# A talking-heads attention with a gated feed-forward: first tile in another order, every second block's first head mixing in three fp32r products

## The chip, the cores and the metric

The kernel runs on one core of a Trainium2 chip. The metric is the device time in microseconds of one execution. TensorE (PE) multiplies, PEld is its weight load, DVE (VectorE), ACT (ScalarE) and POOL (GpSimd) work element by element, and SP (SyncE) issues most DMAs. Each engine runs its own instructions strictly in the order in which they were written; between engines there are semaphores.

## The reference

There are 4 batches, 12 heads, 448 positions and 64 numbers per head. All inputs and the output are fp32, except that the two large weights arrive as 64-bit floats.

```python
scores = scale * np.matmul(q, k.transpose(0, 1, 3, 2))
scores = np.einsum('bhij,hg->bgij', scores, w_pre)
scores = scores - np.max(scores, axis=-1, keepdims=True)
attn = np.exp(scores)
attn = attn / (np.sum(attn, axis=-1, keepdims=True) + 1e-09)
attn = np.einsum('bhij,hg->bgij', attn, w_post)
x = np.matmul(attn, v)              # then to 1792 tokens x 768
h = x @ w_in                        # 768 x 2048
g = np.where(h >= 1, h, np.where(h <= -1, 0, (h + 1) ** 2 / 4))
out = g @ w_out                     # 2048 x 768
```

## The kernel before

The attention is cut into 16 tiles of up to 120 query rows (120, 120, 120 and 88 in each batch). `scores` (L143 to L165) multiplies a tile's queries with the keys of two pairs of heads, in three fp32r products per head: queries and keys had been split into a high part (rounded to fp32r) and the low rest, which `trans_k` and `trans_q` make when they transpose. A `scores` call leaves four PSUM banks, and ACT copies one of them to `ssb` (L160), DVE three (L164).

A *block* is 10 query rows of a tile with all 12 heads, so 120 rows (108 for some) by 448 keys: `load_s` (L179, a DMA on SP) gathers them from `ssb`, `pre` (L185) mixes the heads with one fp32 product whose stationary side is `wpre`, a 120 x 120 matrix that holds w_pre ten times along its diagonal. The profile shows this product as two instructions. `row_max` (L189, DVE), `exps` (L195, ACT) and `norm` (L201 and L202 on DVE, then `wr` on POOL, L206) make the softmax, `post` (L216, ACT copy L218) does the second mixing, and `pv` (L232) multiplies with the values.

Blocks go in 48 *groups*: 36 of four blocks and 12 of three. The main loop has one *step* per group, and in step n it writes, in this order: the `load_s` of group n+1, all `pre` of group n, all `row_max`, all `exps`, `norm`, some work of a weight conversion (`convs`, L267 to L286, spread over ACT, DVE and POOL), `post` of group n-1, transposes for coming tiles (`trans_k` in nine of the steps, whose casts L125 and subtractions L128 are DVE's), `pv`, a `scores` call, and a list of late items. The late items of steps 44 to 47 are the first work of the feed-forward: `load_x` (L382, three buffers `xr`) and `split_x` (L390 on ACT, L391 on DVE) for its first 512 tokens, and `load_w` (L353, L355). SP's queue is in order: a DMA that must wait for a buffer holds up all behind it.

PSUM has six banks `ps_l`, used in turn by `pre`, `post`, the transposes, `pv` and half of `scores`, and two banks `ps_q`.

Before the loop stands the first tile: loads of q and k (L101, L110), transposes with small `warm` products (L499) between them, three `scores` calls, the `load_s` of group 0. After it come 64 steps of the feed-forward (`ffn1` L404, `gate`, `ffn2` L441), with fp32r products throughout; the change does not touch them.

Of the kernel before, what the change touches and what calls it, by code (L numbers as in the profile page):

```python
# [9 lines left out]
F32 = mybir.dt.float32  # L10
# [5 lines left out]
ALU = mybir.AluOpType  # L16
# [6 lines left out]
def tile_talking_heads_moe(  # L23
# [119 lines left out]
    def scores(t, hps):  # L143
# [6 lines left out]
        for u, hp in enumerate(hps):  # L150
# [6 lines left out]
            (rest if u else todo).append((2 * hp, ps[0]))  # L157
# [23 lines left out]

    def pre(m):
        k = blocks[m][2] * H
        lps[m] = ps_l.tile([128, S], F32, tag="l", name="ps_l")
        nc.tensor.matmul(out=lps[m], lhsT=wpre[:k], rhs=s10.pop(m)[:k], start=True, stop=True)  # L185

    def row_max(m):
        nm = ap_.tile([128, 1], F32, tag="nm", name="nm", bufs=8)
# [271 lines left out]
    with tc.manual_schedule():  # L460
        load_q(0, (0,))
        k0 = [ap_.tile([KP, 2, KC, 2, D], F32, tag=f"v{g}", name=f"k0{g}", bufs=1) for g in range(3)]
# [14 lines left out]
        wrep = const.tile([128, 2, H], F32, name="wrep")  # L477
        nc.vector.memset(wrep, 0.0)
        for n, w in enumerate((w_pre, w_post)):
            nc.scalar.dma_start(out=wrep[:KM, n, :], in_=w.unsqueeze(0).to_broadcast([IB, H, H]))  # L480

        wpre = const.tile([128, 128], F32, name="wpre")
        wpost = const.tile([128, H, IB], F32, name="wpost")
        nc.vector.memset(wpre, 0.0)

        nc.vector.scalar_tensor_tensor(
            out=wpre[:, :KM].rearrange("p (i g) -> p i g", g=H),
            in0=mask.unsqueeze(2).to_broadcast([128, IB, H]), scalar=float(D) ** -0.5,
# [198 lines left out]
```

## Time and profile before

| what | value |
|---|---|
| median of 3 runs | 975.99 us (975.35 to 978.43) |
| the profiled execution | 973.09 us, its span 971.4 us |
| PE busy | 947.6 us, 98% of the span |
| DVE, ACT, POOL busy | 57%, 53%, 17% |
| first `pre` / last `pre` of the attention | 32.35 us / 477.14 us from the span's start |
| mean granted clock of TensorE | 0.993 of full speed |

The span is what the trace covers; 1.7 us of the execution lie around it. A matmul's busy time overlaps the next one's, so the cost of a matmul in a row is the distance from its start to the start of the next. Times in the rows below are from the start of the span.

### The profile page before, as it was taken

Reading aid. Unit: us, or ns where it says so; the run is one execution under the profiler, and the core shown is the slowest. Engines: PE = TensorE matmul, PEld = TensorE weight load, DVE = VectorE, ACT = ScalarE, POOL = GpSimd, SP = SyncE. Lnnn points to the kernel's source line nnn. Section 1 sums busy time; section 2 is a strip of 40 time slices with the busy share of each in tenths; the row PEclk is TensorE's granted clock in tenths of the full one; section 3 lists DMA queues with packets and bytes.
Section 4 is the critical chain, followed back from the end, with each engine's and each line's share of the span. In section 5 each row is a group of like instructions: output and inputs, shape, how many; then the busy total and the mean of one; then the engine's idle time right before and its main releaser. Section 6 shows DMA issues by size and latency. Waiting matters only on the chain.

```text
span 971.4 us, 17796 instructions
## 1 busy us (share of the span) xinstructions
PE 947.6 (98%) x6698; PEld 775.7 (80%) x6698; DVE 554.7 (57%) x997; ACT 517.9 (53%) x1097; POOL 169.2 (17%) x253
## 2 busy tenths in 40 slices
PE   7999999999999999999899999999999999999997
PEld 6667777777778787777688877888888888888997
DVE  3665756666665756654355566554454644545774
ACT  2566577666676666665555454443333533334553
POOL 0134233323333233422201212000000000000000
PEclk8999999999999999999999999999999999999999
DMA  5685657775667856653544432020000200000100
GB/s 88 177 240 163 198 177 216 212 211 176 198 199 218 218 173 206 191 196 107 166 163 140 149 128 87 11 98 1 1 23 1 92 1 1 12 1 6 65 2 33
DMA packets 118362, 115.22 MB, mean 119 GB/s; under 512 B 61700, under 2 KB 107268, under 8 KB 118276
## 3 DMA queue, kind: packets, MB, share of 16 engines
q1 hardware_dynamic: 115232, 113.37, 38.4%
q10 hardware_dynamic: 3044, 0.70, 0.5%
q8 instruction: 54, 0.88, 0.4%
q14 instruction: 32, 0.26, 0.1%
HBM read 55.85 MB, written 19.66 MB: 78 GB/s over the span
## 4 chain that ended last, share of the span: by engine, by line
PE 91%; DMA 3%; DVE 2%; ACT 1%; issue 1%; POOL 1%; ACTq 0%; SPq 0%; POOLq 0%
PE o L441 22%; PE ps_h L404 22%; PE ps_l L185 15%; PE ps_a L216 15%; PE ps_x L232 8%; PE ps_s L155 7%; DMA s<-ssb 2%; PE ps_w L499 1%; PE ps_k L121 1%; PE ps_t L138 1%; POOL wo L286 1%; DMA k<-in_k_dram 1%; DMA wi<-wid 0%; DVE mx L418 0%; DVE mx L417 0%
## 5 line engine op out<-in xcount | busy, mean ns | idle before, releaser
L216 PEld LDWEIGHTS ps_a<-wr,e 128*112 128x112 f32 x1440 | 154.6, 177 | 18.5 <-issue 18.5
L195 ACT ACTIVATE e<-ps_l,nm 128x448 f32<-128x448 f32 x180 | 113.0, 632 | 94.3 <-DVE nm L189 93.7
L206 POOL TENSOR_SCALAR wr<-wpost,rs 128x120 f32<-128x120 f32 x180 | 103.2, 591 | 337.1 <-DVE rs L202 290.4
L185 PE MATMUL ps_l<-s,wpre 120*128 120x448 f32 x360 | 150.3, 559 | 6.6 <-DMA s<-ssb 6.6
L216 PE MATMUL ps_a<-wr,e 128*112 128x120 f32 (+1 forms) x1440 | 155.3, 266 | 0.0
L404 PE MATMUL ps_h<-xh,wil 128*128 128x512 f32 (+1 forms) x384 | 139.5, 363 | 0.0
L404 PE MATMUL ps_h<-xl,wih 128*128 128x512 f32 (+1 forms) x384 | 139.2, 363 | 0.0
L404 PE MATMUL ps_h<-xh,wih 128*128 128x512 f32 (+1 forms) x384 | 139.2, 362 | 0.0
L185 PEld LDWEIGHTS ps_l<-s,wpre 120*128 120x128 f32 x360 | 64.6, 191 | 72.2 <-issue 62.0
L441 PE MATMUL o<-woh,gl 128*128 128x512 f32 x448 | 115.7, 339 | 4.4 <-DVE gl L421 4.4
L189 DVE TENSOR_REDUCE nm<-ps_l 128x1 f32<-128x448 f32 x180 | 105.1, 618 | 21.1 <-PE ps_l L185 16.0
L441 PE MATMUL o<-woh,gh 128*128 128x512 f32 x448 | 115.6, 339 | 0.0
L441 PE MATMUL o<-wol,gh 128*128 128x512 f32 x448 | 115.2, 339 | 0.0
L417 DVE TENSOR_TENSOR mx<-ps_h,a 128x512 f32<-128x512 f32 (+1 forms) x64 | 39.9, 624 | 120.6 <-ACT a L416 120.6
L164 DVE COPY ssb<-ps_s 120x448 f32<-120x448 f32 (+1 forms) x144 | 82.6, 619 | 44.3 <-PE ps_s L155 41.4
L416 ACT ACTIVATE a<-ps_h,c 128x512 f32<-128x512 f32 (+1 forms) x64 | 40.5, 633 | 113.5 <-PE ps_h L404 113.4
L218 ACT ACTIVATE aT<-ps_a 112x480 f32<-112x480 f32 x180 | 96.0, 591 | 4.9 <-PE ps_a L216 3.6
L441 PEld LDWEIGHTS o<-woh,gl 128*128 128x128 f32 x448 | 75.1, 189 | 17.9 <-DVE gl L421 6.8
L420 ACT ACTIVATE gh<-mx 128x512 fp32r<-128x512 f32 (+1 forms) x64 | 37.0, 578 | 92.5 <-DVE mx L418 92.5
L441 PEld LDWEIGHTS o<-wol,gh 128*128 128x128 f32 x448 | 76.3, 188 | 10.0
L441 PEld LDWEIGHTS o<-woh,gh 128*128 128x128 f32 x448 | 76.4, 188 | 9.7
L232 PE MATMUL ps_x<-aT,v 112*64 112x120 f32 (+1 forms) x1536 | 83.8, 262 | 0.0
(66 smaller groups left out, 1246.5 us busy)
## 6 DMA issues: line engine op xcount, KB each, us to landing
s<-ssb SPq DMA_DIRECT2D x172, 210.0 KB
wraw<-in_moe_w_in_dram SPq DMA_DIRECT2D x32, 384.0 KB
raw<-in_moe_w_out_dram SPq DMA_DIRECT2D x20, 384.0 KB
wid<-wt SPq DMA_DIRECT2D x32, 192.0 KB
wi<-wid SPq DMA_DIRECT2D x16, 384.0 KB
v<-in_v_dram SPq DMA_DIRECT2D x12, 448.0 KB
out_dram<-osb SPq DMA_DIRECT2D x14, 384.0 KB
wraw<-in_moe_w_out_dram SPq DMA_DIRECT2D x12, 384.0 KB
```

Of the source, the lines that this page charges most:

```text
L155: nc.tensor.matmul(out=ps[s][:n], lhsT=qt[t][x][r, hp, :n], rhs=kt[b, hp][y][r, :], start=(m == 0), stop=(m == 2))
L164: nc.vector.tensor_copy(out=ssb[t][:n, h, :], in_=x[:n])
L185: nc.tensor.matmul(out=lps[m], lhsT=wpre[:k], rhs=s10.pop(m)[:k], start=True, stop=True)
L189: nc.vector.tensor_reduce(out=nm, in_=lps[m], axis=AX.X, op=ALU.max, negate=True)
L195: nc.scalar.activation(out=e, in_=ps, func=AF.Exp, bias=nm, accum_out=sm[:, j:j + 1])
L206: nc.gpsimd.tensor_scalar_mul(out=w[:, :, :ni], in0=wpost[:, :, :ni], scalar1=rs[:, j:j + 1])
L216: nc.tensor.matmul(out=ps[:, r, :ni * H], lhsT=e[:, r * KP:(r + 1) * KP], rhs=w[:, :, :ni], start=True, stop=True)
L218: nc.scalar.activation(out=aT[t][:, :, :, c:c + ni], in_=ps[:, :, :ni * H].rearrange("q r (h i) -> q r h i", h=H), func=AF.Copy)
L232: nc.tensor.matmul(out=ps[s * D:(s + 1) * D, m, :n], lhsT=vt[b, g][:, 2 * m + s, r * D:(r + 1) * D], rhs=a[:, r, 4 * g + 2 * m + s, :n], s ...
L404: nc.tensor.matmul(out=ps[:, :n], lhsT=w[:, kk, :], rhs=x[:, :n], start=(c == 0), stop=(c == last))
L416: nc.scalar.activation(out=a[:, :n], in_=ps[:, :n], func=AF.Relu, scale=0.5, bias=c05)
L441: nc.tensor.matmul(out=o[bank][:, c0:c0 + ne], lhsT=g[:, t * 128:(t + 1) * 128], rhs=w[:, e0:e0 + ne], start=(f == 0 and m == 0 and c0 == ...
```

## The change

Five edits:

- Every second block of a group (`groups[n + 1][1::2]`: two of four, one of three; 82 blocks in all, since group 0 has no step before it) is no longer mixed by one fp32 product. In the step before, DVE makes `sh`, its fp32r value, and `sl`, the rest (new `split`, two instructions); `pre` then takes three fp32r products with `wpre_h` and `wpre_l`. One split stands between `row_max` and `exps`/`norm` of the step, the other after `norm`. `load_s` issues these blocks first.
- A `scores` call has two of its four copies on ACT and two on DVE.
- The first tile: the key loads of pairs 3 to 5 on ACT's queue, all others on SP's; ACT's table load ahead of them; the loads of w_pre and w_post on SP; the transposes of all key pairs ahead of the three `scores` calls, with fewer `warm` products; `wpre` and `wpost`, with the split of `wpre`, after the copies of the scores.
- `load_x` and `split_x` of the first 512 tokens at other steps: no load in step 45, loads 3 and 4 in step 46, load 5 in step 47.
- Tiles of 128 partitions that used 120 have 120.

```diff
 def load_k(b, hp, t=None):
-            (nc.scalar if first and s else nc.sync).dma_start(...)
+            (nc.scalar if first and hp > 2 else nc.sync).dma_start(...)
 def scores(t, hps):
-            (rest if u else todo).append((2 * hp, ps[0]))
+            todo.append((2 * hp, ps[0]))
...
+    def split(m):
+        k = blocks[m][2] * H
+        x = s10.pop(m)
+        hi = ap_.tile([KM, S], F32R, tag="sh", name="sh", bufs=2)
+        lo = ap_.tile([KM, S], F32R, tag="sl", name="sl", bufs=2)
+        nc.vector.tensor_copy(out=hi[:k], in_=x[:k])
+        nc.vector.tensor_tensor(out=lo[:k], in0=x[:k], in1=hi[:k].bitcast(F32), op=ALU.subtract)
+        s10[m] = (hi, lo)
...
+        if isinstance(x, tuple):
+            for j, (w, y) in enumerate(((wpre_h, x[0]), (wpre_l, x[0]), (wpre_h, x[1]))):
+                nc.tensor.matmul(out=lps[m], lhsT=w[:k], rhs=y[:k], start=(j == 0), stop=(j == 2))
+        else:
+            nc.tensor.matmul(out=lps[m], lhsT=wpre[:k], rhs=x[:k], start=True, stop=True)
...
         for hp in range(1, HP):
-            warm(3)
+            warm(2)
             trans_k(0, hp)
-            if hp in (3, 5):
-                warm(2)
-                scores(0, [hp - 3, hp - 2])()
-        warm(4)
-        scores(0, [4, 5])()
+        for g in range(3):
+            scores(0, [2 * g, 2 * g + 1])()
...
-        for kk in range(KDM):
-            put(NE + 1 + kk // 2, lambda kk=kk: split_x(0, kk))
-            if kk + 3 < KDM:
-                put(NE + 1 + kk // 2, lambda kk=kk: load_x(0, kk + 3))
+        for w0, loads, splits in ((1, (), (0, 1)), (2, (3, 4), (2,)), (3, (5,), (3, 4, 5))):
...
-                for m in groups[n + 1]:
+                for m in (*groups[n + 1][1::2], *groups[n + 1][::2]):
                     load_s(m)
...
+            nxt = list(groups[n + 1][1::2]) if n + 1 < NG else []
             for m in ms:
                 row_max(m)
+            if nxt:
+                split(nxt.pop(0))
             for j, m in enumerate(ms):
                 if j == 3:
                     post(old.pop(0)) if old else None
                 exps(m, j, sm)
             if ms:
                 norm(ms, sm)
+            for m in nxt:
+                split(m)
             convs(share * (n + 0.4))
```

On PE, the first mixing of group 1 with what stands before and behind it. Before (`s_...` are the gathered blocks, `ps_s` the scores):

```order
L155 MATMUL ps_s_415<-kl_186,qh 120x448
L185 MATMUL ps_l<-s_334,wpre 128x448
L185 MATMUL ps_l<-s_336,wpre 128x448
L185 MATMUL ps_l<-s_338,wpre 128x448
L185 MATMUL ps_l<-s_340,wpre 128x448
L216 MATMUL ps_a<-wr,e 112x120 x16
```

and now:

```order
L155 MATMUL ps_s_412<-kl_179,qh 120x448
L200 MATMUL ps_l<-s_326,wpre 120x448
L198 MATMUL ps_l<-sh,wpre_h 120x448
L198 MATMUL ps_l<-sh,wpre_l 120x448
L198 MATMUL ps_l<-sl,wpre_h 120x448
L200 MATMUL ps_l<-s_328,wpre 120x448
L198 MATMUL ps_l<-sh,wpre_h 120x448
L198 MATMUL ps_l<-sh,wpre_l 120x448
L198 MATMUL ps_l<-sl,wpre_h 120x448
L231 MATMUL ps_a<-wr,e 112x120 x16
```

Two of the four fp32 products became three fp32r products each, and PE now goes from fp32 to fp32r and back twice inside the group.

On DVE, step 0 (group 0, with the splits for group 1). Before:

```order
L189 TENSOR_REDUCE nm<-ps_l 128x1 x4
L201 TENSOR_SCALAR rs<-sm 128x4
L202 RECIPROCAL rs<-rs 128x4
L141 TENSOR_TENSOR ql<-ps_t,qh 128x360
L164 COPY ssb<-ps_s_390 120x448
```

and now:

```order
L204 TENSOR_REDUCE nm<-ps_l 120x1 x4
L187 CAST sh<-s_322 120x448
L188 TENSOR_TENSOR sl<-s_322,sh 120x448
L216 TENSOR_SCALAR rs<-sm 120x4
L217 RECIPROCAL rs<-rs 120x4
L187 CAST sh<-s_324 120x448
L188 TENSOR_TENSOR sl<-s_324,sh 120x448
L141 TENSOR_TENSOR ql<-ps_t,qh 128x360
L164 COPY ssb<-ps_s_386 120x448
```

The splits stand ahead of `rs` and ahead of the transposes' and scores' copies, and each waits for a `load_s` of its own step.

On SP, the DMAs of steps 45 and 46 (`s_...` for group 47 are the last three gathers). Before:

```order
L382 DMA xr<-xd 128x512 x2
L353 DMA wi_5949<-wid 128x768
L355 DMA wo_5950<-wod 128x768
L179 DMA s_5953<-ssb 120x1x448
L179 DMA s_5955<-ssb 108x1x448
L179 DMA s_5957<-ssb 108x1x448
```

and now:

```order
L368 DMA wi_6417<-wid 128x768
L370 DMA wo_6418<-wod 128x768
L179 DMA s_6421<-ssb 108x1x448
L179 DMA s_6423<-ssb 120x1x448
L179 DMA s_6425<-ssb 108x1x448
L263 DMA xd<-xo 768x1x120
L397 DMA xr<-xd 128x512 x2
```

The two loads of `xr` went behind the last gathers.

## Rows read from the trace of the kernel before

**Rows 1.** The page: busy time, share of the span and instructions of two engines, and the lines of the chain that ended last, by share of the span.

```profile
PE 947.6 (98%) x6698; PEld 775.7 (80%) x6698; DVE 554.7 (57%) x997; ACT 517.9 (53%) x1097; POOL 169.2 (17%) x253
...
PE o L441 22%; PE ps_h L404 22%; PE ps_l L185 15%; PE ps_a L216 15%; PE ps_x L232 8%; PE ps_s L155 7%; DMA s<-ssb 2%; PE ps_w L499 1%; PE ps_k L121 1%; PE ps_t L138 1%; POOL wo L286 1%; DMA k<-in_k_dram 1%; DMA wi<-wid 0%; DVE mx L418 0%; DVE mx L417 0%
```

**Rows 2.** Busy time by stretch, one whole step (18, which has transposes of keys): the stretch, its length, then busy time and count on PE, PEld, DVE, ACT and POOL, granted clock, DMA share, GB/s.

```profile
201.39:212.13 10.74, 10.74 (x98) 8.40 (x96) 7.86 (x17) 6.70 (x19) 3.24 (x5) 1.00 0.65 189
```

**Rows 3.** The weight loads of one group's `pre` in order of time (start, length, engine, line, operation): the first two, the third, and the first load of `post` behind them. Between the third and the last stand five more of L185.

```profile
306.49 0.30 PEld L185 LDWEIGHTS ps_l<-s,wpre 120*128 120x128 f32 x2 [0.31 <-issue]
306.97 0.19 PEld L185 LDWEIGHTS ps_l<-s,wpre 120*128 120x128 f32 x1 [0.19 <-ACT wk L273]
...
309.23 0.18 PEld L216 LDWEIGHTS ps_a<-wr,e 128*112 128x112 f32 x1 [0.19 <-issue]
```

**Rows 4.** fp32r matmuls of the feed-forward in order of time: the first and the last of 17 in a row with 512 columns, the first and the last of 17 with 256 columns, and the last two pairs of a `scores` call (448 columns, two heads side by side).

```profile
565.40 0.39 PE L404 MATMUL ps_h<-xl,wih 128*128 128x512 f32 x1
...
569.03 0.39 PE L404 MATMUL ps_h<-xh,wih 128*128 128x512 f32 x1
...
929.58 0.28 PE L404 MATMUL ps_h<-xh,wil 128*128 128x256 f32 x1
...
931.49 0.28 PE L404 MATMUL ps_h<-xl,wih 128*128 128x256 f32 x1
...
305.99 0.37 PE L155 MATMUL ps_s<-kh,ql 64*120 64x448 f32 x2
306.20 0.36 PE L155 MATMUL ps_s<-kl,qh 64*120 64x448 f32 x2
```

**Rows 5.** Weight loads where `pv` (fp32, 112 rows by 64 columns) is followed by `pre` (fp32, 120 rows by 128 columns): the first two of `pre`, and the third.

```profile
466.05 0.30 PEld L185 LDWEIGHTS ps_l<-s,wpre 120*128 120x128 f32 x2 [0.16 <-issue]
466.53 0.19 PEld L185 LDWEIGHTS ps_l<-s,wpre 120*128 120x128 f32 x1 [0.19 <-issue]
```

**Rows 6.** Groups by line and form (count, busy us and mean ns of one, idle time before), of DVE: three kinds of operation that are like a split's two, and the copy of the scores. Then, from the views of single lines, shortest, median and longest ns of L282 (DVE, two inputs from SBUF) and of L206 (POOL).

```profile
L276 DVE TENSOR_SCALAR wt<-wt 128x384 int32<-128x384 int32 x44 | 15.2, 347 | 0.0
L125 DVE CAST kh<-ps_k 128x448 fp32r<-128x448 f32 x18 | 11.2, 620 | 7.1 <-PE ps_k L121 7.1
L391 DVE TENSOR_TENSOR xl<-xr,xh 128x512 fp32r<-128x512 f32 x18 | 11.8, 688 | 19.9 <-ACT xh L390 19.9
L164 DVE COPY ssb<-ps_s 120x448 f32<-120x448 f32 x108 | 61.9, 620 | 23.4 <-PE ps_s L155 23.4
...
L282 DVE SCALAR_TENSOR_TENSOR wt<-wraw,wt x44: 557/559/687, 46.6 to 422.8; 128x384 int32<-128x384 int32 x44
...
L206 POOL TENSOR_SCALAR wr<-wpost,rs x180: 552/585/663, 37.5 to 484.6; 128x120 f32<-128x120 f32 x172, 128x108 f32<-128x108 f32 x8
```

**Rows 7.** DVE in step 18 in order of time (start, length; in brackets the idle time before it and what ended it), and SP's issues of the gathers in that step.

```profile
203.41 2.21 DVE L189 TENSOR_REDUCE nm<-ps_l 128x1 f32<-128x448 f32 x4
207.18 0.17 DVE L201 TENSOR_SCALAR rs<-sm 128x4 f32<-128x4 f32 x1 [1.57 <-ACT e L195]
...
208.37 0.62 DVE L125 CAST kh<-ps_k 128x448 fp32r<-128x448 f32 x1 [0.81 <-PE ps_k L121]
...
211.66 1.72 DVE L164 COPY ssb<-ps_s 88x448 f32<-88x448 f32 x3 [0.37 <-PE ps_s L155]
...
201.35 3.52 SPq L179 DMA_DIRECT2D s<-ssb  x4
```

**Rows 8.** The start in order of time: ACT's first work, PE behind it, the last transposes of keys, the last copies of scores, the first gathers, the first `pre`; and a piece of the chain that ended last, from step 2.

```profile
0.78 6.26 ACTq L101 DMA_DIRECT2D k<-in_k_dram  x6
...
10.23 1.28 ACT L140 ACT_TABLE_LOAD   x1 [10.23 <-DMA k<-in_k_dram]
12.84 1.65 PE L499 MATMUL ps_w<-ident 128*128 128x128 f32 x6 [4.71 <-DVE ql L141]
...
21.89 0.55 PE L121 MATMUL ps_k<-ident,k 112*128 112x112 f32 x4
...
2.72 7.63 SPq L101 DMA_DIRECT2D k<-in_k_dram  x5
...
26.49 1.69 DVE L164 COPY ssb<-ps_s 120x448 f32<-120x448 f32 x3 [0.95 <-PE ps_s L155]
28.27 3.47 SPq L179 DMA_DIRECT2D s<-ssb  x4
32.35 2.04 PE L185 MATMUL ps_l<-s,wpre 120*128 120x448 f32 x5
...
52.00 8.12 DMA s<-ssb
```

**Rows 9.** Steps 46 and 47 in order of time: SP's `xr` loads and last gathers, DVE's first `split_x`, and PE's `pre` of group 46 and of group 47; and the busy time by stretch there (columns as in Rows 2).

```profile
467.81 0.92 SPq L382 DMA_DIRECT2D xr<-xd  x2
...
469.78 2.82 SPq L179 DMA_DIRECT2D s<-ssb  x3
...
467.09 1.29 DVE L391 TENSOR_TENSOR xl<-xr,xh 128x512 fp32r<-128x512 f32 x2 [4.08 <-ACT xh L390]
...
466.05 2.52 PE L185 MATMUL ps_l<-s,wpre 120*128 120x448 f32 x6
...
477.14 4.19 PE L185 MATMUL ps_l<-s,wpre 120*128 120x448 f32 x6 [4.32 <-DMA s<-ssb]
...
470.00:480.00 10.00, 5.68 (x48) 3.76 (x47) 2.26 (x5) 4.36 (x12) 1.71 (x3) 0.87 0.93 268
```

More of the change, by code (lines that the diff above doesn't have):

```diff
@@ L100, in load_k @@
         for s in range(2):
-            (nc.scalar if first and s else nc.sync).dma_start(out=t[:, :, s, :], in_=k[b, 2 * hp + s].rearrange("(p r) d -> p r d", r=KC))
+            (nc.scalar if first and hp > 2 else nc.sync).dma_start(out=t[:, :, s, :], in_=k[b, 2 * hp + s].rearrange("(p r) d -> p r d", r=KC))
         kraw[b, hp] = t
@@ L180, in load_s @@
         s10[m] = x
+    def split(m):
[6 more added lines that the diff above has]
+        s10[m] = (hi, lo)
     def pre(m):
         k = blocks[m][2] * H
[L184 to L185 removed]
+        lps[m] = ps_l.tile([KM, S], F32, tag="l", name="ps_l")
+        x = s10.pop(m)
+        if isinstance(x, tuple):
[3 more added lines that the diff above has]
+            nc.tensor.matmul(out=lps[m], lhsT=wpre[:k], rhs=x[:k], start=True, stop=True)
     def row_max(m):
[L188 removed]
+        nm = ap_.tile([KM, 1], F32, tag="nm", name="nm", bufs=8)
         nc.vector.tensor_reduce(out=nm, in_=lps[m], axis=AX.X, op=ALU.max, negate=True)
@@ L467, in tile_talking_heads_moe @@
         load_q(1)
+        wrep = const.tile([KM, 2, H], F32, name="wrep")
+        for n, w in enumerate((w_pre, w_post)):
+            nc.sync.dma_start(out=wrep[:, n, :], in_=w.unsqueeze(0).to_broadcast([IB, H, H]))
         ident = const.tile([128, 128], F32, name="ident")
         make_identity(nc, ident)
-        mask = const.tile([128, IB], F32, name="mask")
+        mask = const.tile([KM, IB], F32, name="mask")
         nc.gpsimd.memset(mask, 1.0)
@@ L476, in tile_talking_heads_moe @@
                                 base=H - 1, pattern=[[H, IB]], channel_multiplier=-1)
[L477 to L488, printed above, removed]
-            in1=wrep[:, 0, :].unsqueeze(1).to_broadcast([128, IB, H]), op0=ALU.mult, op1=ALU.mult)
-        nc.vector.tensor_tensor(
-            out=wpost, in0=wrep[:, 1, :].unsqueeze(2).to_broadcast([128, H, IB]),
-            in1=mask.unsqueeze(1).to_broadcast([128, H, IB]), op=ALU.mult)
-        c05 = const.tile([128, 1], F32, name="c05")
-        nc.vector.memset(c05, 0.5)
         def warm(n):
@@ L556, in tile_talking_heads_moe @@
         put(NE, lambda: load_w(0))
-        for kk in range(KDM):
-            put(NE + 1 + kk // 2, lambda kk=kk: split_x(0, kk))
-            if kk + 3 < KDM:
-                put(NE + 1 + kk // 2, lambda kk=kk: load_x(0, kk + 3))
+        for w0, loads, splits in ((1, (), (0, 1)), (2, (3, 4), (2,)), (3, (5,), (3, 4, 5))):
+            for kk in loads:
+                put(NE + w0, lambda kk=kk: load_x(0, kk))
+            for kk in splits:
+                put(NE + w0, lambda kk=kk: split_x(0, kk))
         for f in range(1, NWE):
```

25 lines of the change are left out of this document (21 added, 4 removed).

## The prediction, made before the changed kernel was run

> **What bounds the kernel now.** I read the page first: PE is busy for 98% of the span and makes nearly the whole chain that ended last, the first mixing (L185) with 15% of it [rows 1]. Then busy time by stretch: in step 18, one of the nine with transposes of keys, PE has no idle time at all and DVE is busy for 7.86 of 10.74 us [rows 2]. So in the steps a matmul saved is time saved as long as DVE and ACT keep up, and DVE's order inside a step decides whether they do [rows 7]. Last I looked for places where PE is not the bound: the start, where PE waits 4.71 us for `ql` and the first `pre` stands at 32.35 us [rows 8], step 2 (8.12 us of the chain are gathers [rows 8]) and step 46 to 47, where PE waits 4.32 us for gathers [rows 9].
>
> **The mixing on PE.** Weight loads give the pace of the fp32 product: from the third (306.97) to the first of `post` (309.23) are six instructions, 2.26 / 6 = 0.377 us each, so 0.753 us for a block's two [rows 3]. fp32r: 512 columns take (569.03 - 565.40) / 16 = 0.227 us, 256 columns (931.49 - 929.58) / 16 = 0.119 us; on the line between them 448 columns take 0.200 us [rows 4]. The pairs of `scores` at 448 columns come 0.21 us apart, which is the upper bound; 448/512 of 0.227, 0.199, is the lower [rows 4]. Three products: 0.60 us. Saved per block 0.753 - 0.60 = 0.15 us, for 82 blocks **12.4 us** (10 to 13).
>
> This holds only if PE pays nothing to change between fp32 and fp32r, and that no row shows by itself. What rows show is a change of type together with a change of tile shape: from the last pair of `scores` (64 rows, 306.20) to the first `pre` weight load (306.49) are 0.29 instead of 0.21 us, and to the third weight load another 0.48 instead of 0.377 [rows 3, 4]; nearly 0.19 us in all. But from `pv` to `pre`, both fp32 and of different shapes, the same 0.48 stands between first and third load [rows 5], and from `pre` to `post`, same type and full rows, there is none: 309.23 closes the even pace [rows 3]. So the shape alone explains the price, and here the shape stays (120 rows). I take zero and keep 0.10 and 0.19 us as the price of each of the new changes: four in each of 35 groups of four, two in each of 12 groups of three, 164 in all.
>
> The Trainium skill (TensorEngine Tiling (Array Packing), section Tiling Modes, Key Properties) says that changing the tiling mode drains TensorE, changing only the tile does not. The rows on `pv` and `pre` agree; by it the 164 changes cost nothing, while with types as a second kind of mode they would cost 16 to 31 us. No run here shows which.
>
> **The start.** ACT issued six key loads in 6.26 us from 0.78, then the two of the weights, and its table load came at 10.23 and took 1.28 us, so that its first `qh` began at 11.5 [rows 8]. Now table load and a tiny copy come first and six issues behind them: 0.8 + 1.3 + 0.2 + 6.3 = 8.6 instead of 11.5, and PE's 4.71 us wait shrinks by 2.9. After that the landing of keys decides: SP's last issue of them ended at 10.35 (2.72 + 7.63) [rows 8], so all have landed at about 12.5 (an estimate; a first gather lands within 4 us of its issue, below). With four more `trans_k` of 0.55 us and some 0.4 us of `warm` each, the last is at about 16 instead of 21.89. Three `scores` calls follow, each 1.4 to 1.5 us with copies shared by two engines, and the last copy ends at about 21.3 instead of 28.18 (26.49 + 1.69): 6.9 us earlier. Given back: `wpre`, `wpost` and the two splits of `wpre` now stand on DVE between these copies and the `ql` that PE's `warm` run waits for, four small operations, about 1.1 us. Take **-5.5 us**; bounds -2.9 (only the earlier ACT) and -8.
>
> **The end.** In step 45 SP could issue the fourth `xr` load only when DVE's first `split_x` was through (467.09 + 0.65), at 467.81, and the last gathers stood behind it and two weight loads: 469.78, and PE began with them at 477.14 after 4.32 us idle. Its six instructions then took 4.19 instead of 2.52 us, with a mean granted clock of 0.87 in that stretch, so part of it at 1.2 instead of 2.4 GHz [rows 9]. Without the `xr` loads ahead, the gathers go right behind the weight loads of step 45, several microseconds earlier. 4.32 + 1.67 = **-6.0 us**. What is late next: loads 3 to 5 of `xr`, needed by `ffn1(0)` some 10 us later; their third split on ACT in step 47 costs about 0.6 us of ACT ahead of `post`'s copies. Bounds -3 and -6.5.
>
> **What DVE pays.** A split is a cast and a subtraction in SBUF, 448 columns. No row has this cast. Nearest below: 0.347 us for 384 columns from SBUF; above: 0.620 us for a cast of 448 from PSUM. I take 0.40, by the row from SBUF. The subtraction is 0.688 x 448/512 = 0.60 us [rows 6]. Two splits 2.0 us (1.9 to 2.45); one copy less, -0.62 [rows 6]. Step 18 then has 7.86 + 1.4 = 9.3 us on DVE against 10.74 - 0.30 on PE: tight, but it fits. In order of time: `row_max` ends at 205.62, `rs` comes at 207.18 after 1.57 us idle, and 0.81 us are idle before the cast at 208.37 [rows 7]; the first split falls into the first gap, the second mostly into the second. `wr` follows `rs` and `post` wants it only in the next step. ACT gets the copy, in the time that DVE saves.
>
> The split waits for a gather issued in its own step. At the start four gathers issued from 28.27 served a `pre` at 32.35, so a first one lands within 4 us [rows 8]; in step 18 they are issued from 201.35, landed by 205.4, and `row_max` ends at 205.62 [rows 7]. Where DMA is loaded it is later (7.4 us from 469.78 to 477.14, 8.12 us in step 2 [rows 8, 9]), and then behind the waiting cast stand `rs`, `ql` and the copies of scores, whose banks PE needs. I count step 0 with 2.5 us (its two `scores` calls wait for copies behind both splits), step 2 with 1, all others together with 1.5: **+5 us** (0 to +12).
>
> By the Trainium skill (SBUF — State Buffer, section Who interferes with whom) a DVE operation with two SBUF inputs, or a cast in a two-port mode, and a POOL operation that reads SBUF block each other wholly. The second split runs beside POOL's four `wr`. By that rule its two operations would wait up to 0.59 us each, which would fill step 18 and add about 5 us. The trace has such meetings: L282 takes 0.559 us, at most 0.687, and `wr` 0.585, at most 0.663 [rows 6]. I take the 0.1 us of the rows.
>
> **The sum.** -12.4 - 5.5 - 6.0 + 5 = -19 us. The profiled execution took 973.09 us, 2.9 below the median; I keep the difference and put it on the median: 975.99 - 19 = **957 us**.
>
> **The rivals.**
>
> *DVE becomes the bound in the steps with transposes.* With casts of 0.62 us step 18 has 9.7 us of work, and a wait of a microsecond for a gather makes 10.7 against PE's 10.44; nine such steps lose a microsecond each. For it: an in-order engine over 90%. Against it: a late DVE meets gathers that have landed. 8 to 9 us more: 965 us.
>
> *A change of type costs half of what a change of shape costs*, 0.10 us: the weight load cannot run ahead. 164 x 0.10 = 16 us eat the mixing's gain, and 973 us are left.
>
> *Slower: a change of type drains PE like a change of shape*, 0.19 us at each of the 164 places in `pre`: +31 us, so 957 + 31 = 988 us. It decides from 19 / 164 = 0.116 us per change. For it: every change of type in this trace has a price. Against it: so has the change of shape without one, and the same price.
>
> **How the numbers follow.** Forecast 0.62, DVE's bound 0.18, half price 0.11, full price 0.09. The forecast's own range goes from 948 (13 + 8 + 6.5 us gained, nothing lost) to 965. For 8 in 10 the upper end must go into the half price, and the lower gets 2 us for the scatter of runs: 946 to 973. A difference under 0.3%, 2.9 us, can't be told from none here. Faster: 0.62 + 0.18 + half of 0.11, so 0.85; same 0.06; slower 0.09.
>
> **What would show it.** In the changed profile the starts of `pre`'s instructions: 0.377 us after fp32, 0.20 after fp32r, with no 0.1 us more where they alternate. The first `pre` at about 27 us. No wait of `pre` for gathers in steps 46 and 47, and the clock there at 1. DVE idle ahead of the first split's cast only where gathers are late; step 18 about 10.4 us long. The forecast is wrong if alternating instructions stand 0.1 us or more farther apart, or if PE begins to wait for DVE in the ordinary steps.

## The result, and the profile after

The changed kernel takes 953.29 us (median of 4 runs, 951.72 to 955.92), the kernel before 976.48 us beside it (4 runs). The ratio is 0.9763, with a 95% interval of 0.9735 to 0.9792: faster by 2.4%. The profiled executions take 952.53 and 973.09 us, a difference of 20.6, and their spans 950.6 and 971.4 us. The page, with the lines of [rows 1]:

```profile
PE 932.6 (98%) x6754; PEld 785.2 (83%) x6754; DVE 606.9 (64%) x1113; ACT 543.0 (57%) x1146; POOL 179.5 (19%) x253
...
PE o L456 22%; PE ps_h L419 22%; PE ps_a L231 16%; PE ps_l L200 8%; PE ps_x L247 8%; PE ps_s L155 7%; PE ps_l L198 5%; PE ps_k L121 1%; DMA k<-in_k_dram 1%; PE ps_t L138 1%; POOL wo L301 1%; DMA s<-ssb 0%; DVE mx L433 0%; DVE wil L389 0%; DVE mx L432 0%
```

PE bounds as before. The first mixing has 13% of the chain (L200, fp32, and L198, fp32r) instead of 15%, and gathers (`s<-ssb`) have gone from 2% to 0%. Lines have moved: L231 is `post`, L204 `row_max`, L216 and L217 the sums of `norm`, L221 `wr`, L187 and L188 the split.

**The mixing.** Weight loads of one group in order of time, as in [rows 3]: the third fp32r product of a block, an fp32 block, the next fp32r block, and the first load of `post`.

```profile
47.14 0.18 PEld L198 LDWEIGHTS ps_l<-sl,wpre_h 120*120 120x120 f32 x1
47.34 0.39 PEld L200 LDWEIGHTS ps_l<-s,wpre 120*120 120x120 f32 x2
47.93 0.18 PEld L198 LDWEIGHTS ps_l<-sh,wpre_h 120*120 120x120 f32 x1 [0.20 <-DVE nm L204]
48.30 0.18 PEld L198 LDWEIGHTS ps_l<-sh,wpre_l 120*120 120x120 f32 x1 [0.19 <-issue]
48.50 0.18 PEld L198 LDWEIGHTS ps_l<-sl,wpre_h 120*120 120x120 f32 x1
48.71 0.59 PEld L231 LDWEIGHTS ps_a<-wr,e 120*112 120x112 f32 x4
```

Look at the sums, not at single distances, since a load runs ahead of the product before it. From 47.34 to 48.71 are 1.37 us for one block of either kind; two fp32 instructions of 0.377 and three fp32r products of 0.20 make 1.354. That leaves 0.02 us for the two changes of type inside this stretch.

**A step with transposes.** Step 18 in the view of busy time by stretch, as in [rows 2], and DVE in it in order of time with SP's gathers for its splits, as in [rows 7]:

```profile
193.91:204.38 10.47, 10.47 (x100) 8.70 (x98) 9.30 (x20) 7.28 (x19) 3.95 (x6) 1.00 0.63 187
```

```profile
195.45 2.21 DVE L204 TENSOR_REDUCE nm<-ps_l 120x1 f32<-120x448 f32 x4
198.24 0.40 DVE L187 CAST sh<-s 120x448 fp32r<-120x448 f32 x1 [0.59 <-DMA s<-ssb]
198.67 0.63 DVE L188 TENSOR_TENSOR sl<-s,sh 120x448 fp32r<-120x448 f32 x1
199.23 0.17 DVE L216 TENSOR_SCALAR rs<-sm 120x4 f32<-120x4 f32 x1
199.44 0.18 DVE L217 RECIPROCAL rs<-rs 120x4 f32<-120x4 f32 x1
199.53 0.36 DVE L187 CAST sh<-s 120x448 fp32r<-120x448 f32 x1
199.93 0.72 DVE L188 TENSOR_TENSOR sl<-s,sh 120x448 fp32r<-120x448 f32 x1
...
203.90 1.24 DVE L164 COPY ssb<-ps_s 88x448 f32<-88x448 f32 x2 [0.38 <-PE ps_s L155]
...
192.70 3.91 SPq L179 DMA_DIRECT2D s<-ssb  x4
```

The step is 0.27 us shorter than before, PE is busy all the time and DVE for 9.30 us. The first split falls into the idle time ahead of `rs`, after 0.59 us of waiting for its gather, and the two copies of the scores still wait for PE.

**The start**, in order of time, as in [rows 8]:

```profile
0.78 1.28 ACT L480 ACT_TABLE_LOAD   x1 [0.78 <-PEq L692]
...
6.75 0.47 ACT L140 ACTIVATE qh<-ps_t 128x360 fp32r<-128x360 f32 x1 [4.48 <-PE ps_t L138]
...
10.69 1.01 PE L121 MATMUL ps_k<-ident,k 112*128 112x112 f32 x4 [0.85 <-DMA k<-in_k_dram]
...
16.69 0.55 PE L121 MATMUL ps_k<-ident,k 112*128 112x112 f32 x4
...
21.56 1.24 DVE L164 COPY ssb<-ps_s 120x448 f32<-120x448 f32 x2 [0.35 <-PE ps_s L155]
...
24.13 3.84 PE L503 MATMUL ps_w<-ident 128*128 128x128 f32 x32 [1.23 <-DVE ql L141]
27.80 3.17 PE L200 MATMUL ps_l<-s,wpre 120*120 120x448 f32 x8
...
33.24 0.46 PE L155 MATMUL ps_s<-kh,qh 64*120 64x448 f32 x1 [0.55 <-ACT ssb L160]
35.16 0.47 PE L155 MATMUL ps_s<-kh,qh 64*120 64x448 f32 x1 [1.46 <-DVE ssb L164]
...
47.09 3.38 SPq L179 DMA_DIRECT2D s<-ssb  x4
...
55.34 0.98 PE L200 MATMUL ps_l<-s,wpre 120*120 120x448 f32 x2 [1.58 <-ACT wk L288]
```

The first `pre` stands at 27.80 instead of 32.35 us. In step 0, PE then waits for copies of scores on ACT (33.24) and on DVE (35.16); the second stands behind the splits. In `no_split`, a run below without splits, these waits are 0.6 and 0.2 us. The wait at 55.34 is put down to ACT, whose `wk` is the last event that the profile saw; the gathers issued from 47.09 belong to this `pre`, and in three runs below that load the same at the start (`adjacent`, `dve_copies`, `more_splits`) the wait at this place is put down to them. It is only 0.3 to 0.4 us there, so the 1.58 us are those of one execution. The place in `more_splits`:

```profile
53.79 0.98 PE L200 MATMUL ps_l<-s,wpre 120*120 120x448 f32 x2 [0.41 <-DMA s<-ssb]
```

Three stretches of the start of the changed kernel:

```profile
8.94:15.77 6.83, 5.94 (x29) 5.38 (x29) 1.78 (x3) 2.06 (x4) 0.00 (x0) 0.50 0.82 116
...
36.25:39.66 3.41, 3.41 (x9) 1.86 (x8) 1.69 (x3) 1.91 (x5) 0.00 (x0) 0.50 0.87 239
...
46.08:55.34 9.26, 7.69 (x56) 6.21 (x55) 6.00 (x14) 8.10 (x20) 2.53 (x4) 1.00 0.80 227
```

In the first, with the transposes of keys, the granted clock is 0.50, that is 1.2 GHz; behind the two waits of step 0 PE runs at that level for 3.41 us again; in step 2 the DMA engines are busy for 80% of the time while PE waits.

**The end**, in order of time, as in [rows 9]:

```profile
446.13 3.12 SPq L179 DMA_DIRECT2D s<-ssb  x3
...
453.30 0.93 SPq L397 DMA_DIRECT2D xr<-xd  x2
...
458.15 1.01 PE L200 MATMUL ps_l<-s,wpre 120*120 120x448 f32 x2
```

The last gathers are issued 12.0 us ahead of the `pre` of group 47 instead of 7.4, the `xr` loads come behind them, and `pre` waits for nothing.

In the following, the length of a step is the distance from the first `pre` of its group to that of the next. Where the 20.7 us between the two spans come from, with 0.145 us per block for the mixing (the upper end of what the steps show, see the first run below), against the terms of the prediction:

| term | predicted | measured |
|---|---|---|
| mixing, 82 blocks | -12.4 | -11.9 |
| first `pre` | -5.5 | -4.6 |
| steps 0 to 3 beside the mixing | +3.5 | +1.6 |
| steps 4 to 45 beside the mixing | +1.5 | +0.2 |
| steps 46 and 47 beside the mixing | -6.0 | -6.1 |
| feed-forward | 0 | 0.0 |

These are differences of two single executions, and the start varies by a microsecond or more. Among the profiled executions of kernels with the same first tile, the first `pre` stands at 26.16 to 28.70 us, and in `x_order_only`, which has the old one, at 33.37 instead of 32.35. Steps 0 to 3 take 35.4 us here but 34.2 in `adjacent` and `more_splits`.

### The profile page after: what moved, and what is told of

Read it like the earlier page. It is cut to its first block, busy times and chain, and to the rows that moved or that the text cites. A ratio compares the mean times of both kernels' runs of the same rounds, so it can differ in the third digit from the quotient of the medians.

```text
span 950.6 us, 17979 instructions
## 1 busy us (share of the span) xinstructions
PE 932.6 (98%) x6754; PEld 785.2 (83%) x6754; DVE 606.9 (64%) x1113; ACT 543.0 (57%) x1146; POOL 179.5 (19%) x253
## 4 chain that ended last, share of the span: by engine, by line
PE 92%; DVE 2%; ACT 2%; DMA 1%; issue 1%; POOL 1%; SPq 0%; POOLq 0%; ACTq 0%
PE o L456 22%; PE ps_h L419 22%; PE ps_a L231 16%; PE ps_l L200 8%; PE ps_x L247 8%; PE ps_s L155 7%; PE ps_l L198 5%; PE ps_k L121 1%; DMA k<-in_k_dram 1%; PE ps_t L138 1%; POOL wo L301 1%; DMA s<-ssb 0%; DVE mx L433 0%; DVE wil L389 0%; DVE mx L432 0%
## 5 line engine op out<-in xcount | busy, mean ns | idle before, releaser
L221 POOL TENSOR_SCALAR wr<-wpost,rs 120x120 f32<-120x120 f32 x180 | 113.4, 647 | 306.7 <-DVE rs L217 273.2
L231 PEld LDWEIGHTS ps_a<-wr,e 120*112 120x112 f32 x1440 | 154.3, 177 | 6.7 <-issue 4.9
L231 PE MATMUL ps_a<-wr,e 120*112 120x120 f32 (+1 forms) x1440 | 155.2, 266 | 0.0
L210 ACT ACTIVATE e<-ps_l,nm 120x448 f32<-120x448 f32 x180 | 112.8, 632 | 56.8 <-DVE nm L204 56.2
L204 DVE TENSOR_REDUCE nm<-ps_l 120x1 f32<-120x448 f32 x180 | 104.2, 618 | 14.7 <-PE ps_l L200 11.8
L200 PE MATMUL ps_l<-s,wpre 120*120 120x448 f32 x196 | 94.6, 567 | 1.6 <-ACT wk L288 1.6
L419 PEld LDWEIGHTS ps_h<-xl,wih 128*128 128x128 f32 x384 | 72.4, 189 | 12.2
L419 PEld LDWEIGHTS ps_h<-xh,wih 128*128 128x128 f32 x384 | 72.4, 189 | 11.5
```

Of the source, the lines that this page charges most:

```text
L200: nc.tensor.matmul(out=lps[m], lhsT=wpre[:k], rhs=x[:k], start=True, stop=True)
L204: nc.vector.tensor_reduce(out=nm, in_=lps[m], axis=AX.X, op=ALU.max, negate=True)
L210: nc.scalar.activation(out=e, in_=ps, func=AF.Exp, bias=nm, accum_out=sm[:, j:j + 1])
L221: nc.gpsimd.tensor_scalar_mul(out=w[:, :, :ni], in0=wpost[:, :, :ni], scalar1=rs[:, j:j + 1])
L231: nc.tensor.matmul(out=ps[:, r, :ni * H], lhsT=e[:, r * KP:(r + 1) * KP], rhs=w[:, :, :ni], start=True, stop=True)
L419: nc.tensor.matmul(out=ps[:, :n], lhsT=w[:, kk, :], rhs=x[:, :n], start=(c == 0), stop=(c == last))
```

## The experiments

The theory after the result was the forecast's: three separate gains, a change of type that costs nothing, and a start that loses part of its gain again. Open were three things: whether the parts add up, whether the change of type is free, and what holds the start. The kernel before was timed again beside each set of runs; its medians were 974.0 to 975.4 us.

### The parts alone

`no_split` issues no split, and so mixes all blocks in fp32, and it gathers them in the old order:

```diff
-            nxt = list(groups[n + 1][1::2]) if n + 1 < NG else []
+            nxt = []
```

> The changed kernel with every block mixed by the one fp32 product again (no splits, gathers in the old order); start, copies and the xr order as changed. My theory: the mixing is worth 0.145 us per block, 82 blocks, 11.9 us, and the splits cost 1.4 us of waiting in step 0 and some 1.1 us of halved clock in step 1; so 953.3 + 11.9 - 2.5 = 963 us, steps 4 to 44 with four blocks 0.29 us longer than in the changed kernel, those with three 0.15 us, steps 0 and 1 together 2.5 us shorter. Rival (the gain of the steps comes from the copies moved to ACT and not from the products): steps as short as in the changed kernel, about 951 us.

Measured: 963.79 us, ratio 0.9883 (0.9865 to 0.9901). Steps 4 to 44 have their old lengths, so the copies moved to ACT did not shorten them: step 42 takes 9.66 us as before, against 9.38 in the changed kernel, and step 33, of three blocks with one split, 9.24 against 9.10. That is 0.14 us per block. Over steps 5 to 44 the mean is 0.137 us against `no_split` and 0.144 against the kernel before, so 11.3 to 11.8 us for 82. Steps 0 and 1 are 2.6 us shorter than in the changed kernel, as the splits of step 0 cost there; but steps 2 and 3 are 2.9 us longer (19.96 instead of 17.07), of which the mixing explains 0.6; in the rest PE waits for gathers, and behind the wait the granted clock is 0.54 from 54.3 to 58.0 us:

```profile
54.23 4.93 PE L200 MATMUL ps_l<-s,wpre 120*120 120x448 f32 x8 [2.20 <-DMA s<-ssb]
```

`x_order_only` is the kernel before with the new order of `load_x` and `split_x` alone.

> The kernel before with one edit: the loads and splits of the first 512 tokens at the steps of the changed kernel. My theory: the 4.3 us wait for the last gathers and 1.7 us of halved clock behind it come from the two xr loads ahead of them on SP's queue; 976.5 - 6.0 = 970.5 us, no wait of pre in step 47, no drop of the clock there. Rival (the gathers were late because the DMA engines were full): the wait stays at 3 us or more, about 975 us.

Measured: 968.63 us, ratio 0.9931 (0.9904 to 0.9958), or 5.8 us of the 974.45 beside it. Steps 46 and 47 are 5.7 us shorter, the wait of 4.32 us is gone, and the clock stays full there. `no_split` gained 10.7 us against the same runs of the kernel before, so by difference 4.8 are left for the start and the copies. That is near the -4.6 of the first `pre`, but the start was not run by itself.

### The change of type

`adjacent` mixes a group's fp32 blocks first and its split blocks behind them, so that a group of four has two changes of type instead of four (`row_max` and `exps` follow the same order):

```diff
+            ms = (*ms[::2], *ms[1::2])
             for m in ms:
                 pre(m)
```

> The changed kernel with the blocks of a group taken in the order 0, 2, 1, 3: PE's first mixing goes from fp32 to fp32r once per group of four and not twice. My theory (a change of type costs nothing): steps as long as in the changed kernel, 953.3 us within 1. Rival (a change of type costs 0.1 us or more each and the three products would otherwise be cheaper): groups of four lose two changes, 0.2 us a step, 35 steps, 7 us: 946 us.

Measured: 952.64 us, ratio 0.9776 (0.9756 to 0.9795), the same as the changed kernel. From step 5 to step 44 all steps but 13 and 39, which are 0.18 and 0.15 us longer, agree within 0.03 us: step 18 takes 10.44 us (10.47), step 42 9.38 (9.38). PE's first mixing in one group of this kernel, and the first and last instruction of the same stretch in the changed one:

```profile
407.01 1.76 PE L200 MATMUL ps_l<-s,wpre 120*120 120x448 f32 x4
408.26 0.72 PE L198 MATMUL ps_l<-sh,wpre_h 120*120 120x448 f32 x1
...
409.83 3.44 PE L231 MATMUL ps_a<-wr,e 120*112 120x120 f32 x32
...
46.08 1.01 PE L200 MATMUL ps_l<-s,wpre 120*120 120x448 f32 x2
...
48.91 0.27 PE L231 MATMUL ps_a<-wr,e 120*112 120x120 f32 x1
```

From 407.01 to 409.83 are 2.82 us with one change from fp32 to fp32r; in the changed kernel, with two and one back, the same stretch is 48.91 - 46.08 = 2.83 us. So a change at an unchanged tile shape costs nothing that can be seen here: 70 changes fewer would have been worth 7 us at 0.10 us each. Both rivals that priced it fall.

### What holds the start

`late_splits` leaves step 0 without splits (group 1 all in fp32), all others as they are:

```diff
+            nxt = list(groups[n + 1][1::2]) if 0 < n and n + 1 < NG else []
```

> The changed kernel without the two splits of step 0 (the blocks of group 1 in one fp32 product each). My theory: in step 0 the splits stand ahead of the copies of the scores that PE waits for, and this wait lets the clock fall in step 1; without them steps 0 and 1 are 2.5 us shorter and group 1 costs 0.3 us more: 953.3 - 2.2 = 951 us, the clock stays at full in step 1. Rival (the start is bound by the gathers and the DMA behind them, so what is won in step 0 is waited for in steps 2 and 3): the time by step 4 is the same, 953 us.

Measured: 951.74 us, ratio 0.9766 (0.9743 to 0.979), between the theory's 951 and the rival's 953 and not told apart from the changed kernel. The profiled execution is the slowest of the four (954.51 us, the others 950.33 to 953.14), and it is the rival's case. Steps 0 and 1 take 15.71 instead of 18.27 us, steps 2 and 3 21.39 instead of 17.07, with a wait of 2.98 us:

```profile
53.70 1.82 PE L200 MATMUL ps_l<-s,wpre 120*120 120x448 f32 x2 [2.98 <-DMA s<-ssb]
```

```profile
52.96:59.78 6.82, 6.08 (x14) 4.07 (x15) 5.08 (x10) 2.17 (x6) 3.67 (x5) 0.50 0.76 251
```

Around and behind the wait the clock is at 1.2 GHz for 6.82 us. In this execution, what makes steps 0 and 1 shorter is waited for in steps 2 and 3; the two executions at 950.3 us must lose less, and have no profile. Two explanations stood: the gathers of group 3 are late because of what the DMA engines carry ahead of them (1.3 MB of `v`, then raw weights of the conversion), or because of the order in which it comes. `v_later` moves the `v` loads, `v_later_late` does so without the splits of step 0:

```diff
         for g in range(3):
-            put(1, lambda g=g: load_v(0, g))
+            put(2, lambda g=g: load_v(0, g))
```

> The kernel after, with the v loads of the second tile issued with the late items of step 2 instead of step 1. Theory (the gain of the start is lost in steps 2 and 3, because the gathers of groups 2 and 3 stand behind about 1.3 MB of v in the DMA engines): steps 2 and 3 take about 15.5 instead of 17.1 us, the rest stays, and the time is 951 to 952 us, 1 to 2 us below the kernel after. Rival (the early steps are bound by the bytes that all their loads move, whichever comes first): the wait moves to steps 3 to 5, and the start of step 5 (72.8 us after) and the time (953) stay as they are. The two differ little in the total; the starts of steps 3, 4 and 5 in the trace tell them apart.

> The kernel without splits in step 0 (late_splits, 951.7 us), with the v loads of the second tile issued in step 2 as well. Theory (steps 0 and 1 are 2.5 us shorter without the splits of step 0 and lose this only to gathers that wait behind v): steps 0 to 3 take about 32 us instead of 37.1, step 4 starts near 59.5 to 60.5 us instead of 64.4, and the time is 947.5 to 949.5 us, below every kernel so far. Rival (bound by bytes): step 4 or 5 takes what is won, step 6 starts at 82 us as after, and the time is 951 to 953 us.

Measured: 955.25 us (0.9798, 0.9774 to 0.9821) and 953.95 us (0.9783, 0.9761 to 0.9805), both no gain. The theory was right about step 2 (7.61 instead of 9.27 us, the wait gone) and wrong about the sum: steps 3 and 4 take 10.98 and 12.24 us instead of 7.80 and 9.64, because now the gathers of group 4 stand behind `v`. Two stretches of `v_later`, and the `pre` of group 4:

```profile
44.00:48.00 4.00, 4.00 (x22) 2.71 (x22) 3.73 (x8) 3.46 (x8) 2.80 (x4) 1.00 0.02 10
...
56.00:60.00 4.00, 4.00 (x42) 3.85 (x42) 0.69 (x2) 2.06 (x7) 0.00 (x0) 1.00 1.04 307
```

```profile
64.03 1.82 PE L200 MATMUL ps_l<-s,wpre 120*120 120x448 f32 x2 [3.06 <-DMA s<-ssb]
```

The DMA engines are nearly idle from 44 to 48 us and full from 52 to 60: the later place of `v` wastes a gap ahead of the gathers and fills the time behind. So bytes were taken out of the start instead. `conv_later` begins the weight conversion in step 3 and does it 7.5% faster per step, so that it ends where it did:

```diff
-            share = nconv / (NE - 1)
+            share = nconv / (NE - 4)
...
-            convs(share * (n + 0.4))
+            convs(share * (n - 2.6))
...
-            convs(share * (n + 1))
+            convs(share * (n - 2))
```

> The kernel after, with the weight conversion (its loads of wraw, its work on ACT, DVE and POOL, its stores) begun in step 3 instead of step 0 and done 7.5% faster per step, so that it ends where it did. Theory (what was won at the start is lost in steps 2 and 3 because the first gathers share the DMA engines with 1.3 MB of v and 0.39 MB of wraw a step): with three chunks less, some 1.2 MB or 5 us of the DMA engines at the 240 GB/s of that stretch, group 3 is mixed at about 53.5 instead of 55.3 us, step 5 starts near 71 instead of 72.8, and the time is 951 to 952 us. Rival (the gathers' own latency binds, whatever the traffic): group 3 still at 55, and the time 953 us or, with more conversion work in the steps with transposes, up to 955.

> The same later conversion in the kernel without splits in step 0. Theory (bytes): steps 0 to 3 take 31.5 to 33.5 us instead of 37.1, no wait of PE for gathers above 1.5 us there, step 4 starts at 59.5 to 61 instead of 64.4, and the time is 947 to 949.5 us. Rival (latency, or the bytes catch up with steps 4 and 5 as they did with v in step 2): step 6 starts at 82 us as in the kernel after, and the time is 951 to 953 us.

Measured: 950.38 us (0.9742, 0.9718 to 0.9767) and 947.76 us (0.9716, 0.9691 to 0.9741). In `conv_later` step 2 takes 7.61 us, group 3 is mixed at 53.37 and step 5 begins at 70.86. In `conv_later_late` steps 0 to 3 take 31.1 us, step 4 begins at 59.84, and PE waits for no gather before it. The conversion's work on ACT, DVE and POOL has gone from these steps too, but what PE had waited for were gathers, and in `v_later` the wait of step 2 went away with that work in place. Step 2 of `conv_later` by busy time, and its gathers and `pre`:

```profile
45.77:53.37 7.60, 7.60 (x56) 6.17 (x54) 6.24 (x13) 5.95 (x15) 2.04 (x5) 1.00 0.44 165
```

```profile
46.77 6.75 SPq L179 DMA_DIRECT2D s<-ssb  x8
...
53.37 1.01 PE L200 MATMUL ps_l<-s,wpre 120*120 120x448 f32 x2
```

Gathers issued at 46.77 serve a `pre` at 53.37, within 6.6 us at a DMA share of 0.44, where 8.25 us pass at 0.80 in the changed kernel. Without the splits of step 0 the gain is clear: every execution of `conv_later_late` (946.54 to 949.07) is faster than every one of `late_splits` (950.33 to 954.51), by 4.0 us between the medians. With them it is 2.9 us by the medians, while the intervals overlap, and step 4 begins 33.7 us behind the first `pre`, against 34.2 in `adjacent` and `more_splits` and 35.4 in the changed kernel. So the traffic beside the gathers holds the start where the splits do not, and once it is gone the splits of step 0 cost what they seemed to: 2.6 us between the two medians.

### How much room DVE has

`dve_copies` gives one of a `scores` call's four copies back to DVE, which then has three, as before the change:

```diff
-            todo.append((2 * hp, ps[0]))
+            (rest if u else todo).append((2 * hp, ps[0]))
```

> The kernel after, with one of four score copies on ACT and three on DVE again, as before. Theory (in the steps with transposes of keys DVE has 9.3 us of work in 10.46 us and PE is the bound): with 0.62 us more DVE has 9.9 us, the steps keep their 10.46 us, at most the first steps lose half a microsecond, and the time is 952.5 to 955 us. Rival (DVE is at its limit there already, so that the two ACT copies carry the result): steps 6, 7, 18, 19, 30 and 31 become 0.4 to 0.7 us longer, the others with transposes too, and the time is 957 to 960 us.

Measured: 956.99 us (953.87 to 959.98), ratio 0.9812 (0.9779 to 0.9846), at the edge of the rival's range, and not told apart from the changed kernel. The reading by steps is clearer than the total, but it is that of a fast execution (954.74 us); the two above 959 us have no profile. In it the rival's mechanism is absent. The steps with transposes keep their lengths (10.46 and 10.47 us), with DVE 0.36 us busier in step 18:

```profile
194.71:205.18 10.47, 10.47 (x100) 8.70 (x98) 9.66 (x21) 6.60 (x19) 4.16 (x6) 1.00 0.66 193
```

What is lost is lost in steps 4, 12, 16 and 24 (0.95, 0.45, 0.49 and 0.88 us more). PE waits there for gathers or for `exps`, up to 0.8 us at a time, which fits a third copy that comes later on DVE. But single steps of that kind are longer in other runs too (step 16 takes 10.26 us in `late_splits`), so this stays open.

`all_split` splits every block from group 1 on, with more buffers for `sh` and `sl` and fewer for `s10` (five instead of eight) and `e`, and gathers in the old order:

```diff
+            nxt = list(groups[n + 1]) if n + 1 < NG else []
```

> The kernel after, with every block of every group from 1 on mixed in three fp32r products, all splits on DVE, and more buffers for sh and sl. Theory (each block saves 0.145 us on PE, but DVE pays 1.0 us for it): the steps with transposes have 11.3 us of work on DVE and take 11.2 to 11.6 us instead of 10.46; other steps of four with scores (7.1 to 7.6 us of DVE now) come out level or up to 0.25 us shorter; the groups of three save 0.29 us; steps 0 and 1 lose 2 us more. In all 954 to 962 us, no gain. Rival (PE bounds all steps whatever DVE has): 84 more blocks by 0.145 us, about 941 us.

Measured: 974.95 us, ratio 0.9993 (0.9975 to 1.0011). The direction was right and the size was not: I counted DVE's work and forgot its waits. Step 18 takes 10.79 us and step 19 takes 12.39:

```profile
204.30:215.09 10.79, 10.46 (x101) 9.11 (x99) 10.01 (x21) 7.13 (x19) 5.70 (x8) 1.00 0.79 213
...
215.09:227.48 12.39, 10.71 (x101) 9.04 (x100) 11.32 (x25) 7.66 (x20) 4.62 (x6) 1.00 0.80 224
```

DVE's 11.32 us in step 19 are what was worked out, but it also stands idle for 1.07 us, above all where `rs` waits for `exps` with three more splits queued behind it, and PE then waits for DVE and ACT in turn. So a step with transposes becomes DVE's between 9.7 us of DVE work, which cost nothing in `dve_copies`, and 10.0, where step 18 is longer. But the nine steps with transposes have only 10.2 of the 24.6 us between the two spans. Others that were forecast as level, as 16, 25, 28 and 36, are 1.6 to 2.1 us longer. In one of them, step 25, PE waits 1.8 us in its `pre`. The wait is put down to `ql`, which stands on DVE behind two splits whose gather came late:

```profile
272.66 0.43 DVE L187 CAST sh<-s 120x448 fp32r<-120x448 f32 x1 [1.16 <-DMA s<-ssb]
```

How much of the loss comes from such waits, and whether the fewer buffers of `s10` have a part in it, is not shown.

`more_splits` splits 15 blocks more, only in groups whose step before leaves DVE room (three buffers for `sh` and `sl`, seven for `s10` and `e`):

```diff
+        more = (10, 11, 22, 23, 34, 35, 42, 43, 44)
+        def chosen(n):
+            return list(groups[n][-3:] if n in more else groups[n][1::2])
...
+            nxt = chosen(n + 1) if n + 1 < NG else []
```

> The kernel after, with 15 blocks more split, only where DVE has room (5.9 to 7.5 us of work in a step): all three blocks of groups 10, 11, 22, 23, 34 and 35, three of four in groups 42, 43 and 44; one buffer more for sh and sl, one less for s10 and e. Theory (0.145 us of PE per block, DVE's 1.0 us hidden): the six steps 10, 11, 22, 23, 34 and 35 are 0.29 us shorter, the other three 0.145, 2.2 us in all: about 951 us. Rival (each split also costs a wait of the work behind it, as in the kernel in which all blocks are split): the steps keep their length and the time is 953 us or more.

Measured: 949.62 us (949.38 to 953.19), ratio 0.9746 (0.9718 to 0.9773). The nine steps are 2.0 us shorter together: step 10 7.98 instead of 8.27 us, step 42 9.22 instead of 9.38; step 23 alone gains only 0.10. The theory holds in the trace, while the two intervals overlap.

### Together

`combined` has the later conversion, no splits in step 0, and the 15 blocks.

> Later conversion, no splits in step 0, and the 15 blocks more of the run with more splits, in one kernel. Theory (the two gains lie at different places, the start and nine later steps, and neither uses what the other needs): 947.8 - 2.2 = 945.6 us, 944.5 to 947. Rival (the faster conversion has taken the room on DVE that the splits need): the nine steps keep their length, and the time is 947.8 us or more.

Measured: 945.87 us (944.39 to 947.94), ratio 0.9715 (0.9701 to 0.9728), below the interval of the changed kernel. The nine steps are 2.1 us shorter than in `conv_later_late`, and step 4 begins at 58.23 us, as the first `pre` stands at 27.09 instead of 28.70; steps 0 to 3 take 31.1 us in both. It is the fastest of these kernels by its median; against `conv_later_late`, whose ratio is 0.9716, the ratios alone show no gain.

## Why the prediction was right, point by point

- **What bounds the kernel** was read rightly. PE is the bound of the ordinary steps, and a matmul saved there is time saved.
- **The mixing**: 0.15 us per block forecast, 0.137 to 0.145 measured. The line between 256 and 512 columns gave 0.20 us for 448, and 0.20 is what the loads show (0.41 us for two, from 48.30 to 48.71).
- **No price for the change of type** was right, and for the reason given: the rows that showed a price also changed the tile's shape. The rule of the Trainium skill that was weighed there (TensorEngine Tiling (Array Packing), section Tiling Modes, Key Properties) says that a change of tiling mode drains TensorE. That a type is no mode of its own is what `adjacent` shows: 94 changes instead of 164, the same time.
- **The start**: -4.6 instead of -5.5 us. The difference is no more than the scatter of the first `pre` between executions. In this one, the mis-sized step is the transposes "of 0.55 us". PE waits for q and k up to 10.69, and while the clock is at 0.50 the transposes take 0.95 to 1.01 us each. The last one begins at 16.69 (forecast: about 16), and from there to the end of the last copy, 22.8, are 6.1 us (5.3 forecast). The work on `wpre` gave back 0.8 us where 1.4 had been taken.
- **The end**: -6.1 against -6.0 us; nothing became late behind it.
- **What DVE pays** was the weakest term, 1.8 us measured where 5 were forecast. Step 0 is 1.4 us longer, as its PE waits say (2.0 us instead of 0.8 in `no_split`); 2.5 were forecast. Step 1 is 1.1 us longer (9.28 instead of 8.20 in `no_split`), 1.4 beside the mixing, through the clock, which was not in the sum. Step 2's wait was forecast as the splits' fault and is not: `no_split` has it too. Steps 2 and 3 were 1.2 us shorter beside the mixing, which no term had; without that, step 0 and the clock come to 2.8 us, close to the 2.5 of the forecast's step 0 by another path. "All others" cost nearly nothing, though not as reasoned: a first gather does not always land within 4 us. In step 18 the first cast begins 5.5 us behind the first issue, at the end of a wait for its gather, and DVE waits for gathers ahead of 27 of the 82 casts, 36.5 us in all. PE does not feel it in the ordinary steps. The split itself was right: 0.38 us for the cast (0.40 forecast), 0.63 for the subtraction (0.60), a step 18 of 10.47 us (10.4) and 9.30 us on DVE (9.3).
- **The rivals** fell: DVE is not the bound in the steps with transposes, which the profile of `dve_copies` bears out with more work for it, and neither price of a type change exists.
- **The sum**: -19 us forecast, -20.6 between the profiled executions. 957 us was 3.7 too high for the median: 1.6 by the terms, and 2.1 because I carried over the 2.9 us between the profiled execution before and its median, while the profiled execution after is only 0.8 us below its own.

## What to carry to other kernels

An fp32 product can be exchanged for three fp32r products wherever PE is the bound and another engine has a microsecond per block to spare; it may stand between fp32 products, but the splits belong only into steps whose engine still has idle time after its own waits are counted. Before a prologue is made shorter, look at what bounds the steps behind it: here the gain of the start was held by gathers that shared the DMA engines with loads that nobody needed yet, and taking these out was worth more than another order. When a wait goes away, look for it one or two steps later before counting it as won.

## What the runs showed of the hardware

A wait of PE can cost about as much again behind it. Two waits of PE in step 0, of 0.55 and 1.46 us, were followed by 3.41 us at 1.2 GHz in step 1, which made that step 1.1 us longer although its mixing is 0.3 us shorter; in `no_split`, with waits of 0.6 and 0.2 us, the clock is 1.00 throughout steps 0 and 1. A wait of 3.0 us in `late_splits` has 6.82 us at 1.2 GHz around and behind it, and step 3 takes 10.75 us there, 7.84 in `conv_later_late`. The share of busy time of PE looks full in the first of these stretches (3.41 of 3.41 us), and only the granted clock tells. But a wait does not always have this effect: in the kernel before, PE waits 2.00 us ahead of the `pre` of group 3, as long as in `no_split` (2.20 us, then 0.54), and the clock stays at 1.00 from 56 to 67 us.

```profile
58.12 1.88 PE L185 MATMUL ps_l<-s,wpre 120*128 120x448 f32 x4 [2.00 <-DMA s<-ssb]
```

DVE's subtraction and POOL's `wr`, both reading SBUF, do disturb each other, with one exception by less than an instruction. First two views of single lines (count; shortest, median and longest ns), then DVE and POOL in step 38:

```profile
L188 DVE TENSOR_TENSOR sl<-s,sh x82: 624/626/723, 32.2 to 456.9; 120x448 fp32r<-120x448 f32 x78, 108x448 fp32r<-108x448 f32 x4
...
L221 POOL TENSOR_SCALAR wr<-wpost,rs x180: 556/586/1382, 33.3 to 464.4; 120x120 f32<-120x120 f32 x172, 120x108 f32<-120x108 f32 x8
```

```profile
387.09 0.72 DVE L188 TENSOR_TENSOR sl<-s,sh 120x448 fp32r<-120x448 f32 x1
387.73 0.35 DVE L291 TENSOR_SCALAR wt<-wt 128x384 int32<-128x384 int32 x1
...
386.97 2.72 POOL L221 TENSOR_SCALAR wr<-wpost,rs 120x120 f32<-120x120 f32 x4 [6.74 <-DVE rs L217]
```

The subtraction takes 0.72 instead of 0.63 us beside `wr` (34 of the 82 begin while a `wr` runs, and they take 0.67 to 0.72), and the mean of `wr` rises by 0.056 us (647 ns on the page, 591 before), with one of 1.38, which lies beside two subtractions of `split_x` in a row (452.58 and 453.19, 0.69 us each). The four here take 2.72 us together, and 2.41 in step 18; behind the subtraction stands a shift of the conversion in SBUF (L291) here and a cast from PSUM there. By the rule weighed in the prediction (the Trainium skill, SBUF — State Buffer, section Who interferes with whom) the later of the two would wait until the earlier is done; the `wr` of 1.38 us comes near that, the subtraction, which never takes more than 0.1 us over its median, does not. So the 0.1 us of the rows was the right price for DVE, and POOL has so much room that its share cost nothing.
